# Attention scores of a head pair in one burst over four quadrants of TensorE, and a step later for the transposes

## The chip, the cores and the metric

The kernel runs on one core of one Trainium2 chip. The metric is the device time of one execution in microseconds (us), as the median of the runs; the profile shows one further execution. Engines: TensorE (PE; PEld is its weight load), VectorE (DVE), ScalarE (ACT), GpSimd (POOL) and SyncE (SP, which issues the DMAs).

## What is computed

Attention with two kinds of heads, then a feed-forward block with a gate, then a soft mixture of experts. Cut to what matters here:

```python
scores = scale * np.matmul(q, k.transpose(0, 1, 3, 2))      # 4 batches, 8 heads, 576 positions, 64 columns
mask_local   = (rel >= 0) & (rel < 32)                       # heads 0 to 3
mask_strided = (rel >= 0) & (pos[None, :] % 32 == pos[:, None] % 32)   # heads 4 to 7
attn = softmax(where(mask, scores, -1e9))
x = attn @ v                                                 # 2304 tokens, 512 columns
h = x @ w_in;  g = h * sigmoid(1.702 * h);  x = g @ w_out
...                                                          # slots: logits = x @ phi, experts, combination
```

## The kernel before

Everything is written out in Python loops, and the Tile framework gives each engine its fixed order, which follows the order of the calls except where it expects an operand too late.

**Chunks and steps.** The 2304 tokens are worked on in five chunks (four of 512, one of 256). A chunk has 16 steps, one for each 128 columns of the hidden layer. `moe_step` does a step: it advances the generators in `side` by one yield, lets `g_transpose` do 32 x 32 transposes on VectorE, and then `gemm1` (L321) fills the tile h_f with 12 products; ScalarE's tanh (L324) and a multiply on VectorE (L325) make g_f of it. Two h tiles are in PSUM at a time. After step f = 4, 8 and 12 (and step 0 of the next chunk) `logits` (L340) multiplies the last four g tiles. The tail of a chunk (`post`: the products lr, lp and u) runs in the first steps of the next.

**Attention beside it.** Batch b + 1 runs beside chunk b as a generator in `side` (`attention_steps`). A batch has four head pairs: pairs 0 and 1 are local, 2 and 3 strided. The two heads of a pair lie on partitions 0 to 63 and 64 to 127. The allowed positions are cut in units: 9 of 64 queries and 96 keys for a local pair, 11 of 64 x 64 for a strided one. The units are divided in two parts (5 + 4, 6 + 5). For each part `att_scores` computes the products (L163, two for a unit, one a head: row half h of TensorE into column half h), and then the softmax: mask and scale on VectorE (L166, from PSUM), maximum (L176), exponentials one unit at a time on ScalarE (L181), sum and reciprocal (L182, L183), and the normalisation on GpSimd (L184). `att_transpose` (L199) turns the probabilities of a pair on TensorE, and ScalarE copies them out (L203). `att_values` (L218) multiplies with V; ScalarE casts the result into the high part of x (L243), VectorE subtracts to get the low part (L244). For a strided pair the values of part 0 lie in row half 0 and those of part 1 in row half 1.

**The order around the change.** For batches 1 to 3 the sequence of steps is: scores 0.0, 0.1 (pair.part), then alternately the transposes or values of one pair and a score part of the next. Scores 0.0 and 0.1 both come in step 0 of the chunk; after that, a part, a transpose or values come in a step each. K and Q of a pair are loaded before its first part (two buffers), V before its transposes (one buffer). All small PSUM tiles (scores, transposes, values, lr, lp, u) come from the five buffers of `mtile`.

Of the kernel before, what the change touches and what calls it, by code (L numbers as in the profile page):

```python
# [18 lines left out]
B, H, S, D = 4, 8, 576, 64  # L19
# [5 lines left out]
QT, KL, NTL = 64, 96, 9  # L25
QS, KS, NTS = 3 * RA, 64, 11
SW = QS * (NTS - 1) + KS
HS = (NTS + 1) // 2
# [13 lines left out]
def tile_kernel(ctx: ExitStack, tc: tile.TileContext, lqk, lv, sqk, sv, wraw, phi, wexp, cst, out):  # L42
    nc = tc.nc
    P = 128
# [20 lines left out]
    def mtile(name):  # L65
        return ps_m.tile([P, 512], F32, tag="m", name=name)
# [22 lines left out]
    identb = att.tile([P, P], BF16, name="identb", bufs=1)  # L89
    maskb = att.tile([P, C_END - C_ML], BF16, name="maskb", bufs=1)  # L90
    maskL, maskL0, maskS = maskb[:, :KL], maskb[:, KL:2 * KL], maskb[:, 2 * KL:]
# [35 lines left out]

    probs, ptiles = {}, {}

    def att_scores(b, hp, part):  # L130
        t = qkv[b, hp]
        local = hp < 2
        nk, step = (KL, QT) if local else (KS, QS)
        ko = S if local else SW
        total, half = (NTL, 5) if local else (NTS, HS)
        u0, u1 = (0, half) if part == 0 else (half, total)
        nt = u1 - u0
        early = b == 0
        nm = f"{b}_{hp}_{part}"
        if part == 0:  # L140
            shape = [P, NTL if local else 2 * HS, nk]
            if b == 0 and hp >= 2:
                ts = ep.tile(shape, F32, name=f"ts_{b}_{hp}")
            else:
                ts = att.tile(shape, F32, tag="ts", name=f"ts_{b}_{hp}")
            probs[b, hp] = ts
            if not local:
                nc.gpsimd.memset(ts[:, NTS], 0.0)
        if local:
            ts = probs[b, hp][:, u0:u1]  # L150
        else:
            ts = probs[b, hp].rearrange("p (j e) k -> p e j k", e=2)[:, part, :nt]
        sp = mtile(f"s_{nm}")[:, :nt * nk].rearrange("p (u k) -> p u k", k=nk)
        mask = maskL if local else maskS
        if early:
            nc.tensor.matmul(sp, identb, mask.unsqueeze(1).to_broadcast([P, nt, nk]), start=True, stop=False)
            if local and part == 0:
                nc.tensor.matmul(sp[:, 0], identb, maskL0, start=False, stop=False)
        for u in range(nt):
            qo = step * (u0 + u)  # L160
            for h in range(2):
                hs = slice(64 * h, 64 * h + 64)
                nc.tensor.matmul(sp[hs, u], t[hs, qo:qo + 64], t[hs, ko + qo:ko + qo + nk], start=not early, stop=not early or u == nt - 1)  # L163

        def add_mask(a, z, m):
            nc.vector.scalar_tensor_tensor(ts[:, a:z], sp[:, a:z], SCALE, m.unsqueeze(1).to_broadcast([P, z - a, nk]), op0=ALU.mult, op1=ALU.add)  # L166

        if not early:
            if local and part == 0:
                add_mask(0, 1, maskL0)  # L170
                add_mask(1, nt, mask)
            else:
                add_mask(0, nt, mask)
        nmx = att.tile([P, 6], F32, tag="nmx", name=f"nmx_{nm}", bufs=4)
        src, sc = (sp, SCALE) if early else (ts, 1.0)
        nc.vector.tensor_reduce(nmx[:, :nt], src, axis=AX.X, op=ALU.max, negate=True)  # L176
        if early:
            nc.vector.tensor_scalar_mul(nmx[:, :nt], nmx[:, :nt], SCALE)
        sm = att.tile([P, 6], F32, tag="sm", name=f"sm_{nm}", bufs=4)
        for u in range(nt):  # L180
            nc.scalar.activation(ts[:, u], src[:, u], AF.Exp, scale=sc, bias=nmx[:, u:u + 1], accum_out=sm[:, u:u + 1])  # L181
        nc.vector.tensor_scalar_add(sm[:, :nt], sm[:, :nt], 1e-9)  # L182
        nc.vector.reciprocal(sm[:, :nt], sm[:, :nt])  # L183
        nc.gpsimd.tensor_tensor(ts, ts, sm[:, :nt].unsqueeze(2).to_broadcast([P, nt, nk]), op=ALU.mult)  # L184
# [20 lines left out]
    def att_values(b, hp):  # L205
        pt, v = ptiles.pop((b, hp)), vals[b, hp]
        local = hp < 2
        cut = 5 if local else HS
        av = [mtile(f"av_{b}_{hp}_{e}") for e in range(2)]

        def product(u, h):
            e, u0 = (0, u) if u < cut else (1, u - cut)
            if local:
                k0, nk, nq, o, w, p = 0, KL, QT, QT * u0, u, u
            else:
                k0, nk, nq, o, w, p = 64 * e, QS, min(QS, S - QS * u), QS * u0, u0, u0
                nk = nq
            nc.tensor.matmul(av[e][64 * h:64 * h + 64, o:o + nq], v[k0:k0 + nk, P * w + 64 * h:P * w + 64 * h + 64],  # L218
                             pt[k0:k0 + nk, p, 64 * h:64 * h + nq], start=True, stop=True)

        order = range(NTL) if local else [u for j in range(HS) for u in (j, j + HS) if u < NTS]
        for u in order:
            for h in range(2):
                product(u, h)
        for e in range(2):
            for c, (c0, cn) in enumerate(CHUNKS):
                if local:
                    s0 = S * b + QT * cut * e
                    n = QT * (cut, NTL - cut)[e]
                    lo, hi = max(s0, c0), min(s0 + n, c0 + cn)  # L230
                    if lo >= hi:
                        continue
                    src = av[e][:, lo - s0:hi - s0]
                    dsts = [x_tile(c)[k][:, hp, lo - c0:hi - c0] for k in range(2)]
                else:
                    a0, a1 = max(0, (c0 - S * b) // STR), min(RA, (c0 + cn - S * b) // STR)
                    if a0 >= a1:
                        continue
                    r0, nr = (0, 3 * HS) if e == 0 else (3 * HS, STR - 3 * HS)
                    lo = S * b + STR * a0 - c0  # L240
                    src = av[e][:, :RA * nr].rearrange("p (r a) -> p r a", a=RA)[:, :, a0:a1]
                    dsts = [x_tile(c)[k][:, hp, lo:lo + STR * (a1 - a0)].rearrange("p (a r) -> p r a", r=STR)[:, r0:r0 + nr, :] for k in range(2)]
                nc.scalar.copy(dsts[0], src)  # L243
                nc.vector.tensor_tensor(dsts[1], src, dsts[0].bitcast(F32), op=ALU.subtract)  # L244
# [261 lines left out]
    nc.vector.tensor_copy(identb, ident)  # L506
    nc.vector.tensor_scalar_mul(maskb, masks, 1.0 / SCALE)

    def attention_steps(b):
        la = 2 if b else 4  # L510
        order = list(range(la)) + [x for u in range(la, 8) for x in (la - 1 - u, u)] + list(range(la - 9, -9, -1))
        for x in order:
            if x >= 0:
                if b and x % 2 == 0:
                    load_qk(b, x // 2)
                att_scores(b, x // 2, x % 2)
                if b == 0:
                    keep_busy(1)
            else:
                x = -x - 1  # L520
                if x % 2:
                    att_values(b, x // 2)
                else:
                    if b:
                        load_v(b, x // 2)
                    att_transpose(b, x // 2)
                if b == 0:
                    keep_busy(4)
            yield

    for n, _ in enumerate(attention_steps(0)):
        if n in (8, 12):
            load_w(n // 4 - 2)
        if n == 10:
            split(0)
# [9 lines left out]

    for i, (c, f) in enumerate(steps):
        if f == 0 and c < 3:
            side.append(attention_steps(c + 1))
            next(side[-1])
        if (c, f) == (1, 0):  # L550
            raw_es.close()
            accp = acc_es.enter_context(tc.tile_pool(name="accp", bufs=1))
            sp_["p"] = accp
            acc = accp.tile([P, 4, 512], F32, name="acc")
            more = accp.tile([P, 3, 512], F32, name="more")
            slots.update({NF + 3 + k: more[:, k] for k in range(3)})
        if (c, f) == (3, 2):
            att_es.close()
            e1p = ctx.enter_context(tc.tile_pool(name="e1p", bufs=6, side="right"))
            for _ in range(6):  # L560
                load_ex(e1p, "e")
            for e in (1, 0, 1):
                load_ex(xp, f"x{e}")
        if (c, f) == (4, 1):
            for e in range(2):
                load_ex(xp, f"x{e}")
        moe_step(i)
        if (c, f) == (4, 4):
            for k in range(2):
                load_ex(None, gx_tile())  # L570
        if c == 4 and f % 2:
            load_ex(wip, "wi")
# [235 lines left out]
```

## Time and profile before

| | us |
|---|---|
| median of 3 runs | 438.43 (436.42 to 438.57) |
| profiled execution, its time | 439.01 |
| profiled execution, its span | 437.1 |
| PE busy | 411.6 |
| DVE busy | 263.6 |
| ACT busy | 194.1 |
| POOL busy | 77.5 |

The span goes from the first to the last instruction; the execution's own time also holds what lies around it. Busy time of PE counts pipelined products, so its share says that TensorE has work, not that it works at its peak. The mean granted clock is 0.985.

### The profile page before, as it was taken

How to read it: one execution, taken by the hardware profiler on the slowest of the kernel's cores; microseconds unless marked ns; L12 is line 12 of the kernel's file. 1: busy time of each engine (PE TensorE's matmuls, PEld its weight loads, DVE VectorE, ACT ScalarE, POOL GpSimd, SP SyncE). 2: the span in 40 equal slices, each digit the busy share in tenths (PEclk: the TensorE clock that was granted, in tenths of full speed). 3: DMA queues.
4: the chain of work that ended last, by engine and by line, in shares of the span. 5: the costliest groups of instructions: out<-in, count | busy, mean ns of one | idle time of the engine just before them, and what ended most of it. 6: DMA issues, size and time to landing. Idle time of an engine off the chain costs nothing.

```text
span 437.1 us, 10068 instructions
## 1 busy us (share of the span) xinstructions
PE 411.6 (94%) x4085; PEld 280.5 (64%) x4085; DVE 263.6 (60%) x564; ACT 194.1 (44%) x640; POOL 77.5 (18%) x96
## 2 busy tenths in 40 slices
PE   8978998998899999999999999999999999799992
PEld 4646575655467767777676776775777797243681
DVE  2789989998996555555557456546545465422141
ACT  3874867766664653555553436331221222220131
POOL 0454545454531110100110001000000000010000
PEclk9999999999989999999999999999999999899997
DMA  8957677676752130213411101693001899859998
GB/s 253 357 170 243 223 208 251 228 242 218 233 183 76 47 101 1 92 37 97 154 40 60 38 1 37 214 410 147 1 0 39 343 349 329 307 212 427 421 358 255
DMA packets 25614, 80.90 MB, mean 185 GB/s; under 512 B 2144, under 2 KB 9440, under 8 KB 21472
## 3 DMA queue, kind: packets, MB, share of 16 engines
q1 hardware_dynamic: 25568, 80.26, 52.5%
q8 instruction: 32, 0.52, 0.5%
q14 instruction: 14, 0.11, 0.1%
HBM read 71.34 MB, written 8.91 MB: 184 GB/s over the span
## 4 chain that ended last, share of the span: by engine, by line
PE 73%; DVE 8%; ACT 7%; POOL 4%; issue 3%; DMA 2%; SPq 0%; ACTq 0%; POOLq 0%; DVEq 0%
PE h L321 39%; PE u L435 5%; PE s L163 4%; PE lg L340 4%; PE op L671 4%; ACT ts L181 3%; PE hp L641 3%; PE ptp L199 3%; PE av L218 3%; DVE wc L264 2%; POOL ts L184 2%; PE fp L688 2%; POOL wc L262 2%; DVE wc L265 1%; DMA raw<-wraw 1%
## 5 line engine op out<-in xcount | busy, mean ns | idle before, releaser
L321 PE MATMUL h<-x,wi 128*128 128x512 f32 (+1 forms) x960 | 225.2, 381 | 4.3 <-POOL wi L273 1.7
L321 PEld LDWEIGHTS h<-x,wi 128*128 128x128 f32 x960 | 162.2, 189 | 53.8 <-issue 13.8
L325 DVE SCALAR_TENSOR_TENSOR gT<-gT,h 128x512 f32<-128x512 f32 (+1 forms) x64 | 40.6, 634 | 62.1 <-ACT gT L324 61.5
L324 ACT ACTIVATE gT<-h 128x512 f32<-128x512 f32 (+1 forms) x64 | 35.5, 555 | 68.2 <-PE h L321 66.6
L181 ACT ACTIVATE ts<-ts,nmx 128x64 f32<-128x64 f32 (+1 forms) x120 | 41.6, 349 | 28.6 <-DVE nmx L176 28.2
L184 POOL TENSOR_TENSOR ts<-ts,sm 128x384 f32<-128x384 f32 (+2 forms) x32 | 27.9, 872 | 139.2 <-DVE sm L183 65.5
L348 DVE STREAM_TRANSPOSE gT<-gT 128x512 f32<-128x512 f32 (+1 forms) x64 | 41.0, 649 | 0.9
L262 POOL TENSOR_SCALAR wc<-wc 128x512 f32<-128x512 f32 x32 | 25.0, 781 | 29.7 <-ACT wc L261 27.2
L340 PE MATMUL lg<-gT,wp 128*32 128x512 f32 (+1 forms) x128 | 27.2, 564 | 0.3 <-ACT wp L297 0.3
L264 DVE SCALAR_TENSOR_TENSOR wc<-raw,wc 128x512 uint32<-128x512 uint32 x32 | 26.0, 816 | 0.4
L263 DVE TENSOR_SCALAR wc<-wc 128x512 uint32<-128x512 uint32 x32 | 20.3, 635 | 7.9 <-POOL wc L262 7.9
L163 PE MATMUL s<-qk 64*64 64x96 f32 (+1 forms) x552 | 25.0, 235 | 0.0
L163 PEld LDWEIGHTS s<-qk 64*64 64x64 f32 x552 | 20.9, 133 | 6.3 <-issue 5.3
L243 ACT CAST x<-av 128x320 fp32r<-128x320 f32 (+20 forms) x54 | 19.1, 394 | 12.7 <-DVE x L244 9.1
L273 POOL TENSOR_TENSOR wi<-wc,wi 128x512 fp32r<-128x512 f32 x16 | 22.0, 1376 | 14.9 <-ACT wi L272 14.7
L265 DVE SCALAR_TENSOR_TENSOR wc<-raw,wc 128x512 uint32<-128x512 uint32 x32 | 24.4, 763 | 0.3
L261 ACT ACTIVATE wc<-raw 128x512 f32<-128x512 f32 x32 | 21.7, 678 | 4.3 <-DMA raw<-wraw 3.8
L182 DVE TENSOR_SCALAR sm<-sm 128x5 f32<-128x5 f32 (+2 forms) x32 | 6.8, 213 | 27.5 <-ACT ts L181 27.5
L435 PE MATMUL u<-gT,dT 32*32 32x512 f32 x576 | 21.0, 618 | 2.1 <-DVE z L410 2.1
L199 PE MATMUL ptp<-cs,ts 128*96 128x128 f32 (+1 forms) x120 | 18.2, 286 | 4.9 <-POOL ts L184 4.5
L181 ACT ACTIVATION_READ_ACCUMULATOR ts<-ts,nmx 128x1 f32 x120 | 22.6, 188 | 0.0
L699 POOL MEMSET hz<- 128x512 f32 x4 | 2.1, 560 | 112.1 <-PE spp L594 112.1
(124 smaller groups left out, 467.7 us busy)
## 6 DMA issues: line engine op xcount, KB each, us to landing
ex<-wexp SPq DMA_DIRECT2D x28, 1024.0 KB, 8.4
raw<-wraw SPq DMA_DIRECT2D x32, 512.0 KB, 4.2
qk<-lqk SPq DMA_DIRECT2D x8, 592.0 KB, 5.1
wo_scr<-wc SPq DMA_DIRECT2D x16, 256.0 KB, 2.8
ex<-wo_scr SPq DMA_DIRECT2D x4, 1024.0 KB, 9.2
gT<-wexp SPq DMA_DIRECT2D x4, 1024.0 KB, 7.0
qk<-sqk SPq DMA_DIRECT2D x6, 604.0 KB, 4.2
v<-lv SPq DMA_DIRECT2D x8, 432.0 KB, 4.8
```

The source lines that it names most:

```text
L163: nc.tensor.matmul(sp[hs, u], t[hs, qo:qo + 64], t[hs, ko + qo:ko + qo + nk], start=not early, stop=not early or u == nt - 1)
L181: nc.scalar.activation(ts[:, u], src[:, u], AF.Exp, scale=sc, bias=nmx[:, u:u + 1], accum_out=sm[:, u:u + 1])
L184: nc.gpsimd.tensor_tensor(ts, ts, sm[:, :nt].unsqueeze(2).to_broadcast([P, nt, nk]), op=ALU.mult)
L199: nc.tensor.transpose(ptp[:nk, u - a], src, ident)
L262: nc.gpsimd.tensor_scalar(t, t, F64_LARGE, F64_SMALL, op0=ALU.min, op1=ALU.max)
L264: nc.vector.scalar_tensor_tensor(u, raw[:, :, 1], 0xC0000000, u, op0=ALU.bitwise_and, op1=ALU.bitwise_or)
L321: nc.tensor.matmul(h[:, :N], w[:, we, 128 * kt:128 * kt + 128], x[xe][:, kt, :N], start=n == 0, stop=n == 11)
L324: nc.scalar.activation(g[:, :N], h[:, :N], AF.Tanh, scale=0.851)
L325: nc.vector.scalar_tensor_tensor(g[:, :N], g[:, :N], 1.0, h[:, :N], op0=ALU.add, op1=ALU.mult)
L340: nc.tensor.matmul(lgs[c][32 * j:32 * j + 32, :N], wp[:, f0 + j, :], gs[c, f0 + j][:, :N], start=f0 == 0, stop=f0 == NF - 4)
L348: nc.vector.transpose(t_slots(c)[:, f, :N], gs[c, f][:, :N])
L435: nc.tensor.matmul(us[a][32 * j:32 * j + 32, :].rearrange("p (t f) -> p t f", f=32), dT[q, 32 * b:32 * b + 32], gT[q, :, 32 * b:32 * b + 3 ...
```

## The change

- For batches 2 and 3 a new generator `attention_pairs` takes the place of `attention_steps` (now `attention_units`, which still serves batches 0 and 1). Steps of a pair: values of the pair before, scores of both parts, softmax of part 0; softmax of part 1, loads of V and of the next K and Q; a free step (not for pair 3); transposes.
- `att_scores` can issue both parts at once, unit by unit: part 0 and part 1 alternate. Part 1 writes head h into column half 1 - h, so that the four products of a turn use four different quadrants.
- The softmax is a function of its own, `att_softmax`, with the same operations. In part 1 of every batch the heads now stand exchanged in the rows of the probabilities, and so in the columns after the transposes; `att_values` reads them accordingly (`h ^ e`, where e is 1 for the second part of a strided pair).
- K and Q of the first pair of batch 2 are loaded in batch 1's step of the last transposes.

```diff
-    def att_scores(b, hp, part):
+    def att_scores(b, hp, parts=(0, 1)):
...
+        for u in range(half):
+            for part in parts:
+                if part * half + u >= total:
+                    continue
+                qo = step * (part * half + u)
+                for h in range(2):
+                    hs, o = slice(64 * h, 64 * h + 64), 64 * (h ^ part)
+                    nc.tensor.matmul(sp[part][o:o + 64, u], t[hs, qo:qo + 64], t[hs, ko + qo:ko + qo + nk], start=not early, stop=not early or part * half + u in (half - 1, total - 1))
...
-        for u in range(nt):
-            qo = step * (u0 + u)
-            for h in range(2):
-                hs = slice(64 * h, 64 * h + 64)
-                nc.tensor.matmul(sp[hs, u], t[hs, qo:qo + 64], t[hs, ko + qo:ko + qo + nk], start=not early, stop=not early or u == nt - 1)
...
-                             pt[k0:k0 + nk, p, 64 * h:64 * h + nq], start=True, stop=True)
+                             pt[k0:k0 + nk, p, 64 * (h ^ e):64 * (h ^ e) + nq], start=True, stop=True)
...
+                    if (b, x) == (1, 6):
+                        load_qk(2, 0)
...
+    def attention_pairs(b):
+        for hp in range(4):
+            if hp:
+                att_values(b, hp - 1)
+            att_scores(b, hp)
+            att_softmax(b, hp, 0)
+            yield
+            att_softmax(b, hp, 1)
+            load_v(b, hp)
+            if hp < 3:
+                load_qk(b, hp + 1)
+            yield
+            if hp < 3:
+                yield
+            att_transpose(b, hp)
+            yield
+        att_values(b, 3)
+        if b < 3:
+            load_qk(b + 1, 0)
+        yield
...
-            side.append(attention_steps(c + 1))
+            side.append((attention_pairs if c else attention_units)(c + 1))
```

Below is the order of the instructions at three places of batch 2, beside chunk 1. Names: s_pair_part are scores, av values, ptp transposes, pt their copy, ts probabilities, h_f and gT or more the tiles of the gemm, lg the logits, x_2 and x_3 the gemm's operands. In the first two blocks TensorE at step 3. Before, the end of h_3 and what followed it:

```order
L321 MATMUL h_3_1983<-x_1_308,wi_740 128x512
L321 MATMUL h_3_1983<-x_1_307,wi_740 128x512
L163 MATMUL s_1_1_1998<-qk_1_1898 64x96 x8
L435 MATMUL u_0_2018<-gT,dT_1936 32x512 x4
L435 MATMUL u_1_2019<-gT,dT_1936 32x512 x4
```

Now, from the values ahead of h_3 on (the turns go on to the fifth of part 0, and then h_3 comes):

```order
L233 MATMUL av_0_0_1930<-pt_0_1884,v_0_1843 64x64 x10
L233 MATMUL av_0_1_1931<-pt_0_1884,v_0_1843 64x64 x8
L165 MATMUL s_1_0_1959<-qk_1_1845 64x96 x2
L165 MATMUL s_1_1_1960<-qk_1_1845 64x96 x2
L165 MATMUL s_1_0_1959<-qk_1_1845 64x96 x2
L165 MATMUL s_1_1_1960<-qk_1_1845 64x96 x2
```

Part 1 came behind h_3, and part 0 ahead of h_2, a step before the values; now the two parts stand together, in turns, between the values and h_3.

ScalarE in steps 9 to 12, before and now:

```order
L324 ACTIVATE gT<-h_9_2302 128x512
L181 ACTIVATE ts_3_2319,sm_3_0_2337<-ts_3_2319,nmx_3_0_2335 128x64 x6
L324 ACTIVATE gT<-h_10_2348 128x512
L243 CAST x_2_896<-av_2_0_2363 128x18x12
L243 CAST x_2_896<-av_2_1_2364 128x14x12
L243 CAST x_3_1979<-av_2_0_2363 128x18x6
L243 CAST x_3_1979<-av_2_1_2364 128x14x6
L324 ACTIVATE gT<-h_11_2396 128x512
L181 ACTIVATE ts_3_2319,sm_3_1_2425<-ts_3_2319,nmx_3_1_2423 128x64 x5
L324 ACTIVATE more<-h_12_2435 128x512
```

Now:

```order
L339 ACTIVATE gT<-h_10_2320 128x512
L258 CAST x_2_896<-av_2_1_2336 128x14x12
L258 CAST x_2_896<-av_2_0_2335 128x18x12
L258 CAST x_3_1954<-av_2_0_2335 128x18x6
L258 CAST x_3_1954<-av_2_1_2336 128x14x6
L196 ACTIVATE ts_3_2367,sm_3_0_2396<-ts_3_2367,nmx_3_0_2394 128x64 x6
L339 ACTIVATE gT<-h_11_2407 128x512
L196 ACTIVATE ts_3_2367,sm_3_1_2425<-ts_3_2367,nmx_3_1_2423 128x64 x5
L339 ACTIVATE more<-h_12_2437 128x512
```

The six exponentials of part 0 stood ahead of tanh of h_10, a step before the casts; now they stand behind the casts and ahead of tanh of h_11.

TensorE at step 13, before and now:

```order
L340 MATMUL lg_2105<-gT,wp 32x512 x3
L321 MATMUL h_13_2468<-x_1_307,wi_1521 128x512
L321 MATMUL h_13_2468<-x_1_308,wi_1521 128x512
L321 MATMUL h_13_2468<-x_1_307,wi_1521 128x512 x2
L321 MATMUL h_13_2468<-x_1_308,wi_1521 128x512
L199 MATMUL ptp_3_0_2457<-cs,ts_3_2319 128x128 x3
L199 MATMUL ptp_3_1_2462<-cs,ts_3_2319 128x128 x3
```

Now:

```order
L355 MATMUL lg_2109<-gT,wp 32x512 x3
L336 MATMUL h_13_2468<-x_1_307,wi_1521 128x512
L214 MATMUL ptp_3_0_2457<-cs,ts_3_2367 128x128 x3
L214 MATMUL ptp_3_1_2462<-cs,ts_3_2367 128x128 x3
L336 MATMUL h_13_2468<-x_1_308,wi_1521 128x512
```

The transposes of pair 3 stood behind five products of h_13, now behind one (in batch 3 behind three).

## Rows read from the trace of the kernel before

**Rows 1.** The page, part 1: busy time, share of the span, instructions.
```profile
PE 411.6 (94%) x4085; PEld 280.5 (64%) x4085; DVE 263.6 (60%) x564; ACT 194.1 (44%) x640; POOL 77.5 (18%) x96
```

**Rows 2.** Stretches of chunks 1 and 2: busy us of engines, granted clock, DMA share.
```profile
138.20:209.90 71.70, 71.70 (x713) 51.93 (x712) 40.20 (x90) 35.20 (x128) 7.04 (x10) 1.00 0.19 59
209.90:283.00 73.10, 72.93 (x720) 52.89 (x720) 42.13 (x93) 34.08 (x125) 7.04 (x10) 1.00 0.23 75
```

**Rows 3.** Chain of waits in order of time: start, us until the next, what.
```profile
148.30 0.97 PE s L163 x20
...
158.12 0.81 PE s L163 x16
...
171.18 0.84 PE s L163 x24
...
174.97 1.20 PE av L218 x36
176.17 2.95 PE h L321 x12
179.12 0.73 PE s L163 x20
...
182.79 0.99 PE lg L340 x8
```

**Rows 4.** Timeline of PE: start, us, engine, line, operation, count.
```profile
187.44 0.91 PE L163 MATMUL s<-qk 64*64 64x64 f32 x24
...
191.25 0.91 PE L218 MATMUL av<-pt,v 54*64 54x54 f32 x44
192.09 3.01 PE L321 MATMUL h<-x,wi 128*128 128x512 f32 x12
...
201.00 0.87 PE L199 MATMUL ptp<-cs,ts 128*128 128x128 f32 x6
...
209.91 1.70 PE L163 MATMUL s<-qk 64*64 64x96 f32 x36
211.55 3.03 PE L321 MATMUL h<-x,wi 128*128 128x512 f32 x12
```

**Rows 5.** Timeline of ACT, steps 10 to 12 of chunk 1.
```profile
190.48 0.35 ACT L181 ACTIVATE ts<-ts,nmx 128x64 f32<-128x64 f32 x1 [2.34 <-DVE nmx L176]
...
192.49 0.58 ACT L324 ACTIVATE gT<-h 128x512 f32<-128x512 f32 x1
192.97 0.87 ACT L243 CAST x<-av 128x216 fp32r<-128x216 f32 x2
...
197.88 0.35 ACT L181 ACTIVATE ts<-ts,nmx 128x64 f32<-128x64 f32 x1 [2.14 <-DVE nmx L176]
...
199.55 0.58 ACT L324 ACTIVATE more<-h 128x512 f32<-128x512 f32 x1
```

**Rows 6.** Timeline of DVE, steps 10 and 11 of chunk 1.
```profile
188.18 0.69 DVE L325 SCALAR_TENSOR_TENSOR gT<-gT,h 128x512 f32<-128x512 f32 x1 [2.57 <-ACT gT L324]
188.78 0.55 DVE L166 SCALAR_TENSOR_TENSOR ts<-s,maskb 128x384 f32<-128x384 f32 x1
189.25 0.70 DVE L348 STREAM_TRANSPOSE gT<-gT 128x512 f32<-128x512 f32 x1
189.88 0.51 DVE L176 TENSOR_REDUCE nmx<-ts 128x6 f32<-128x384 f32 x1
...
193.10 0.69 DVE L325 SCALAR_TENSOR_TENSOR gT<-gT,h 128x512 f32<-128x512 f32 x1
193.70 0.93 DVE L244 TENSOR_TENSOR x<-av,x 128x216 fp32r<-128x216 f32 x2
...
195.77 0.69 DVE L325 SCALAR_TENSOR_TENSOR gT<-gT,h 128x512 f32<-128x512 f32 x1
```

**Rows 7.** Timeline of POOL, the normalisation of pair 3's part 1 in batch 2.
```profile
200.22 0.72 POOL L184 TENSOR_TENSOR ts<-ts,sm 128x320 f32<-128x320 f32 x1 [6.23 <-ACT more L324]
```

More of the change, by code (lines that the diff above doesn't have):

```diff
@@ L128, in tile_kernel, with att_units @@
     probs, ptiles = {}, {}
-    def att_scores(b, hp, part):
+    sps = {}
+    def att_units(hp):
+        local = hp < 2
+        return (KL, QT, S, NTL, 5, maskL) if local else (KS, QS, SW, NTS, HS, maskS)
+    def att_scores(b, hp, parts=(0, 1)):
         t = qkv[b, hp]
         local = hp < 2
[L133 to L137, printed above, removed]
+        nk, step, ko, total, half, mask = att_units(hp)
         early = b == 0
-        nm = f"{b}_{hp}_{part}"
-        if part == 0:
-            shape = [P, NTL if local else 2 * HS, nk]
+        shape = [P, NTL if local else 2 * HS, nk]
+        if (b, hp) not in probs:
             if b == 0 and hp >= 2:
@@ L148, in att_scores, with att_softmax @@
                 nc.gpsimd.memset(ts[:, NTS], 0.0)
+        sp = sps.setdefault((b, hp), {})
+        for part in parts:
+            nt = (half, total - half)[part]
+            sp[part] = (mtile(f"s_{b}_{hp}_{part}")[:, :nt * nk].rearrange("p (u k) -> p u k", k=nk))
+            if early:
+                nc.tensor.matmul(sp[part], identb, mask.unsqueeze(1).to_broadcast([P, nt, nk]), start=True, stop=False)
+                if local and part == 0:
+                    nc.tensor.matmul(sp[0][:, 0], identb, maskL0, start=False, stop=False)
+        for u in range(half):
+            for part in parts:
+                if part * half + u >= total:
[4 more added lines that the diff above has]
+                    nc.tensor.matmul(sp[part][o:o + 64, u], t[hs, qo:qo + 64], t[hs, ko + qo:ko + qo + nk], start=not early, stop=not early or part * half + u in (half - 1, total - 1))
+    def att_softmax(b, hp, part):
+        local = hp < 2
+        nk, step, ko, total, half, mask = att_units(hp)
+        u0, u1 = (0, half) if part == 0 else (half, total)
+        nt = u1 - u0
+        early = b == 0
+        nm = f"{b}_{hp}_{part}"
+        sp = sps[b, hp][part]
         if local:
@@ L152, in att_scores @@
             ts = probs[b, hp].rearrange("p (j e) k -> p e j k", e=2)[:, part, :nt]
[L153 to L158, printed above, removed]
-        for u in range(nt):
-            qo = step * (u0 + u)
-            for h in range(2):
-                hs = slice(64 * h, 64 * h + 64)
-                nc.tensor.matmul(sp[hs, u], t[hs, qo:qo + 64], t[hs, ko + qo:ko + qo + nk], start=not early, stop=not early or u == nt - 1)
         def add_mask(a, z, m):
@@ L507, in tile_kernel, with attention_units @@
     nc.vector.tensor_scalar_mul(maskb, masks, 1.0 / SCALE)
-    def attention_steps(b):
+    def attention_units(b):
         la = 2 if b else 4
@@ L515, in attention_steps @@
                     load_qk(b, x // 2)
-                att_scores(b, x // 2, x % 2)
+                att_scores(b, x // 2, (x % 2,))
+                att_softmax(b, x // 2, x % 2)
                 if b == 0:
@@ L529, in attention_steps @@
             yield
-    for n, _ in enumerate(attention_steps(0)):
+    def attention_pairs(b):
[18 more added lines that the diff above has]
+        yield
+    for n, _ in enumerate(attention_units(0)):
         if n in (8, 12):
```

## The prediction

> **What bounds the kernel now.** I start with the page: TensorE is busy for 411.6 of 437.1 us [rows 1], so it is the first suspect. An average over the span says nothing of the stage that is changed, so the second view is the table of stretches. Batches 2 and 3 are computed in the stretches from 138.20 and from 209.90 us, beside the gemms of chunks 1 and 2. In the first TensorE is busy for all of its 71.70 us, in the second for 72.93 of 73.10 [rows 2]; VectorE and ScalarE are busy for about half. The granted clock is 1.00 in both, the upper level (2.4 GHz), and as TensorE stays busy I see no reason for it to move. So here a microsecond less of TensorE is one off the end, as long as nothing else becomes late. Later loads of expert weights are released by buffers that TensorE frees, so they move with it.
>
> The third view, the chain of waits in order of time, gives the price of each burst from its start to the next one: 0.84 and 0.73 us for the two score bursts of a strided pair, 0.97 and 0.81 for a local one, 2.95 for the 12 products of an h tile, 0.99 for four logit products, 1.20 for the values of a local pair [rows 3]. The records count double: 22 products of a strided pair show as 24 + 20 records.
>
> The fourth view is TensorE's timeline. The values of a strided pair already go to four quadrants: two row halves (parts 0 and 1) by two column halves (the heads). These 44 records of 54 columns take 0.84 us, from 191.25 to 192.09 [rows 4]. The scores of the same pair use two quadrants, the diagonal, and take 1.57 for 44 records. That contrast is the whole case for the change.
>
> **Part one: the bursts.** Removed: the four strided pairs (two in each of two batches) cost 4 x (0.84 + 0.73) = 6.28 us. Three local pairs cost 0.97 + 0.81 = 1.78 each, and the local pair 0 of batch 3, whose 36 records stand together, takes 1.64 (209.91 to 211.55) [rows 4]; together 6.98. Sum 13.26 us.
>
> Added: the same products in eight bursts over four quadrants. No row has such scores, so I bound them by the values row, 19 ns a record (0.84 / 44).
> - Strided, 64 columns: from 0.84 (if a record costs the same whatever its columns) to 0.84 x 64/54 = 1.00.
> - Local, 96 columns, 36 records: from 36 x 19 ns = 0.69 to 0.69 x 96/54 = 1.22.
>
> Inside these: with two quadrants a record costs 35 ns at 64 columns (0.84 / 24) and 45.6 at 96 (1.64 / 36), so 10.6 more for 32 columns. Four quadrants should show half of that, 5.3 ns. From 54 to 64 columns that adds 1.7 ns (20.8 x 44 = 0.91 us), from 54 to 96 it adds 7 (26 x 36 = 0.94). Sum 4 x 0.91 + 4 x 0.94 = 7.4. **Gain 13.26 - 7.4 = 5.9 us**, by the bounds 13.26 - 8.9 = 4.4 up to 13.26 - 6.1 = 7.1.
>
> Both heads of one part still write into one bank from different row halves, as they do now. Now a record costs 35 ns at 64 columns, and the values of a local pair, which have no row halves and two column halves, cost 33 (1.20 / 36) [rows 3]. So two row halves on one bank show no price. The Trainium skill, "TensorEngine Tiling (Array Packing)", section "Gotcha 1: PSUM Pressure", says that different row tiles cannot access the same bank simultaneously; if they took turns, each of the two banks would serve one row half at a time and the gain would be 0 instead of 5.9. The bursts of now should suffer from that already and do not; its case is rival A.
>
> **Part two: what becomes late.** The softmax of part 0 used to stand a step earlier than that of part 1. Now both follow one burst, ahead of tanh of the h tile of that step on ScalarE, and of the multiply that makes g on VectorE. In step 11 the casts of the values of pair 2 come before both. I walk through step 11 of batch 2, with 0 at the end of h_10.
>
> VectorE: the multiply behind tanh starts 0.74 after TensorE has left the h tile (187.44 to 188.18), the next operation 0.60 later, a transpose takes 0.63 (189.25 to 189.88) [rows 4, 6]; so the subtractions start at 1.97. Four subtractions and a transpose take 2.07 (193.70 to 195.77), so the four take 1.44. The mask of part 0 stands among them, 0.47 (188.78 to 189.25). The maximum starts at 1.97 + 1.44 + 0.47 = 3.88. ScalarE: its exponentials start 0.60 after that (189.88 to 190.48), six take 2.01 (190.48 to 192.49) [rows 5, 6]: 6.49. Then tanh, the multiply 0.61 later (192.49 to 193.10), 0.69 long: g_11 is there at 7.79. TensorE: values 0.84, scores 0.91, two h tiles 5.90: the logits, which need g_11, come at 7.65. **Wait 0.15.** Then the five exponentials of part 1: start 0.48 after tanh did (192.49 to 192.97) at 6.97, 1.67 long (197.88 to 199.55), and 0.67 later GpSimd's normalisation (200.22), 0.72 long [rows 5, 7]: 10.03. TensorE has done the logits at 8.8, and by the new order it comes to the transposes after a single product of h_13, at 9.05. **Wait 1.0.** Before, they stood after five products, and came (201.00) when GpSimd had just finished (200.94).
>
> Batch 3 has all four subtractions and both masks first, so g_11 comes 0.4 later: wait 0.55 at the logits, and at the transposes, after three products of h_13, another 0.55. Sum of these waits 0.15 + 1.0 + 0.55 + 0.55 = 2.25, **taken as 2.3 us**. Bounds: 0, if VectorE or ScalarE overlap the pieces better, and 4.5, if each piece is late by half a microsecond more.
>
> In step 7 there are three subtractions or two of a local pair, not four, and the values take 1.20: by the same steps g_7 comes at about 7.7 and TensorE at 8.0. No wait, with 0.3 to spare. Step 3 has the u products of the chunk before behind h_3, which need nothing of this softmax and cover it; the logits come after them and h_4.
>
> **The rest costs nothing that shows.** The free step lets the transposes of pairs 0 to 2 start a step later, with the softmax long done; it takes away at most the 0.17 us that TensorE shows idle in the second stretch [rows 2]. Splitting the score function changes no instruction. The earlier calls of the loads (in batch 1 too) change no row on SP's queue, and none on GpSimd's; V of a pair still waits for the values of the pair before, three steps ahead of its use. The score tiles take two of five PSUM buffers at once; what held them was read a step earlier, so nobody queues.
>
> **Sum.** The profiled execution took 439.01 us, 437.1 of it span: 439.0 - 5.9 + 2.3 = 435.4. It stands 0.6 above the median of the runs, 438.43; against that the result is **434.9 us**, 0.8% faster.
>
> **Rivals.**
> A. The four quadrants give nothing: the two row halves share each bank and take turns. For it: the values rows have one bank per row half, the scores will not. Against it: the diagonal bursts share a bank at full pace. TensorE then comes to the logits and transposes later by the 0.7 us that the burst did not save (5.9 / 8): the waits at the logits go, and about 0.5 is left at the transposes of each batch, where the order now has them one or three products into h_13 and not five: 438.4 + 1.0 = **439.4 us, slower**. It decides from the point where the eight bursts together save less than 1 us.
> B. The gain is there and the waits are not: the four subtractions are done sooner than I have them, or the bursts end near their upper bound so that TensorE comes later anyway. 438.4 - 5.9 = **432.5 us**.
> C. The gain is there and step 7 stalls like step 11 (spare only 0.3): two waits at the logits of 0.5 and later exponentials, waits 4.5: 438.4 - 5.9 + 4.5 = **437.0 us**, no difference that can be told.
> That the change does not do what it says can be left aside: the order shows the two parts alternating.
>
> **How the numbers follow.** The case of the sum 0.60, B 0.22, C 0.11, A 0.07. A run of this kernel can tell about 0.5% from no change, 2.2 us: the line is 436.2. The sum's own range, with the bounds of the bursts, is 433.4 to 436.4 (the low gain of 4.4 with 2.3 of waits is 436.3), a little of it beyond the line; B lies before it, C beyond, A on the other side but within 0.5% mostly. Faster 0.78, same 0.18, slower 0.04. The range reaches from B with the high gain cut by half a microsecond of waits, 438.4 - 7.1 + 0.5 = 431.8, to C, 437.0.
>
> **What would show it.** Right: the eight bursts show 36 or 44 records in 0.85 to 1.0 us; TensorE waits for the logits after h_12 and for the transposes of pair 3 on GpSimd, some 2 us in all; the stretches of chunks 1 and 2 shrink by 3 to 4 us and later ones keep their length. Wrong: bursts of 1.5 us (A), no idle TensorE in the two stretches (B), a wait for g_7 at the logits after h_8 (C). A stretch of another chunk that changes by more than half a microsecond would be none of my cases.

## The result and the profile after

The changed kernel takes **431.79 us** (median of 4 runs, 430.23 to 433.18), the kernel before 438.28 beside it (4 runs, 436.42 to 438.57). The ratio is 0.9853, with a 95% interval of 0.9828 to 0.9879: 6.5 us faster, where the forecast was 3.5. The forecast range (from 431.8) ends at this time. The profiled execution took 433.18 us, 431.4 of it span, against 439.01 and 437.1.

The page, part 1, answers to [rows 1]:

```profile
PE 403.6 (94%) x4080; PEld 275.2 (64%) x4085; DVE 266.3 (62%) x564; ACT 193.6 (45%) x640; POOL 77.9 (18%) x96
```

TensorE is busy for 8.0 us less, and the span is 5.7 shorter: some of the gain became idle time. To see where, I take one stretch in both traces, from the first score burst of batch 2 to the logits in step 0 of chunk 3. In the kernel before it goes from 138.19 to 284.27, **146.08 us**. Here it is cut in two where batch 3 begins (us, then busy time with the count for TensorE, weight load, VectorE, ScalarE, GpSimd; granted clock; share and rate of the DMAs), and answers to [rows 2]:

```profile
138.00:207.00 69.00, 68.25 (x716) 49.71 (x715) 41.09 (x90) 34.86 (x128) 7.04 (x10) 1.00 0.21 61
207.00:278.74 71.74, 71.04 (x726) 51.55 (x725) 43.82 (x94) 33.84 (x125) 7.04 (x10) 1.00 0.25 83
```

Together **140.74 us**, 5.34 less than before, at the granted clock 1.00 (the upper level) in both. TensorE is idle for 1.45 of it, before for 0.17. So 5.3 of the profiled 5.8 us come from where the change was made.

The new bursts in the chain of waits (start, us until the next, what), which answer to [rows 3]:

```profile
153.07 0.97 PE s L165 x36
...
171.98 1.20 PE av L233 x36
173.18 0.84 PE s L165 x44
174.03 5.66 PE h L336 x24
179.68 1.00 PE lg L355 x8
...
191.59 2.10 ACT ts L196 x12
193.69 0.48 ACT gT L339
194.18 1.67 ACT ts L196 x10
...
196.41 0.72 POOL ts L199
197.18 0.87 PE ptp L214 x6
```

A local pair's 36 records take 0.97 us, a strided pair's 44 take 0.84. The chain leaves TensorE in the lower rows: twelve records of exponentials (six of them), tanh, five more exponentials, the normalisation, and only then the transposes. That is the wait which the prediction walked through, and its two places stand in TensorE's timeline (start, us, engine, line, operation, count, idle time before it and its releaser), as in [rows 4]:

```profile
186.97 0.84 PE L233 MATMUL av<-pt,v 54*64 54x54 f32 x41
...
188.51 5.74 PE L336 MATMUL h<-x,wi 128*128 128x512 f32 x24
194.18 0.62 PE L355 MATMUL lg<-more,wp 128*32 128x512 f32 x1
...
194.64 1.36 PE L355 MATMUL lg<-gT,wp 128*32 128x512 f32 x4
195.92 0.51 PE L336 MATMUL h<-x,wi 128*128 128x512 f32 x1
197.18 0.87 PE L214 MATMUL ptp<-cs,ts 128*128 128x128 f32 x6 [0.75 <-POOL ts L199]
197.81 2.75 PE L336 MATMUL h<-x,wi 128*128 128x512 f32 x11
200.49 0.91 PE L233 MATMUL av<-pt,v 54*64 54x54 f32 x44
...
264.42 1.05 PE L355 MATMUL lg<-gT,wp 128*32 128x512 f32 x2 [0.23 <-DVE gT L340]
265.39 0.96 PE L336 MATMUL h<-x,wi 128*128 128x512 f32 x3
266.65 0.87 PE L214 MATMUL ptp<-cs,ts 128*128 128x128 f32 x6 [0.29 <-POOL ts L199]
```

Idle time alone understates these waits. The logits of step 12 of chunk 1 last from 194.18 to 195.92, 1.74 us, where eight such records take 1.00 elsewhere. Nothing is shown as idle there: records that wait for g_11 are drawn as long ones (1.36). I therefore count a wait as the time from the start of one group to the next, less what the same group takes undisturbed.

### The profile page after: what moved, and what is told of

Read it like the earlier page. It is cut to its first block, busy times and chain, and to the rows that moved or that the text cites. A ratio compares the mean times of both kernels' runs of the same rounds, so it can differ in the third digit from the quotient of the medians.

```text
span 431.4 us, 10062 instructions
## 1 busy us (share of the span) xinstructions
PE 403.6 (94%) x4080; PEld 275.2 (64%) x4085; DVE 266.3 (62%) x564; ACT 193.6 (45%) x640; POOL 77.9 (18%) x96
## 4 chain that ended last, share of the span: by engine, by line
PE 70%; ACT 10%; DVE 9%; POOL 5%; issue 3%; DMA 1%; SPq 0%; ACTq 0%; POOLq 0%; DVEq 0%
PE h L336 37%; ACT ts L196 5%; PE u L450 5%; PE lg L355 4%; PE op L710 4%; PE hp L680 3%; PE s L165 3%; PE ptp L214 2%; POOL ts L199 2%; PE av L233 2%; DVE wc L279 2%; PE fp L727 2%; POOL wc L277 2%; ACT wc L276 1%; DVE x L259 1%
## 5 line engine op out<-in xcount | busy, mean ns | idle before, releaser
L336 PE MATMUL h<-x,wi 128*128 128x512 f32 (+1 forms) x960 | 222.1, 379 | 4.1 <-POOL wi L288 1.7
L355 PE MATMUL lg<-gT,wp 128*32 128x512 f32 (+1 forms) x128 | 28.6, 564 | 0.5 <-ACT wp L312 0.3
L279 DVE SCALAR_TENSOR_TENSOR wc<-raw,wc 128x512 uint32<-128x512 uint32 x32 | 27.0, 845 | 0.4
L280 DVE SCALAR_TENSOR_TENSOR wc<-raw,wc 128x512 uint32<-128x512 uint32 x32 | 24.4, 762 | 0.3
L339 ACT ACTIVATE more<-h 128x512 f32<-128x512 f32 (+1 forms) x16 | 8.6, 536 | 28.2 <-PE h L336 28.2
L259 DVE TENSOR_TENSOR x<-av,x 128x320 fp32r<-128x320 f32 (+20 forms) x54 | 19.9, 392 | 1.8 <-ACT x L258 1.5
L214 PEld LDWEIGHTS ptp<-cs,ts 128*96 128x96 f32 (+1 forms) x120 | 12.8, 132 | 12.8 <-POOL ts L199 11.5
```

The source lines that it names most:

```text
L214: nc.tensor.transpose(ptp[:nk, u - a], src, ident)
L279: nc.vector.scalar_tensor_tensor(u, raw[:, :, 1], 0xC0000000, u, op0=ALU.bitwise_and, op1=ALU.bitwise_or)
L336: nc.tensor.matmul(h[:, :N], w[:, we, 128 * kt:128 * kt + 128], x[xe][:, kt, :N], start=n == 0, stop=n == 11)
L339: nc.scalar.activation(g[:, :N], h[:, :N], AF.Tanh, scale=0.851)
L355: nc.tensor.matmul(lgs[c][32 * j:32 * j + 32, :N], wp[:, f0 + j, :], gs[c, f0 + j][:, :N], start=f0 == 0, stop=f0 == NF - 4)
```

## The experiments

For each, the stretch named above is given beside the time, because it repeats better. In a second profile of the unedited changed kernel it took 140.73 us, against 140.74 in the first, while the two executions took 430.54 and 433.18. Whole runs scatter by 1.5 us and more.

**1. Two quadrants instead of four.**

```diff
-                    hs, o = slice(64 * h, 64 * h + 64), 64 * (h ^ part)
+                    hs, o = slice(64 * h, 64 * h + 64), 64 * h
...
-                             pt[k0:k0 + nk, p, 64 * (h ^ e):64 * (h ^ e) + nq], start=True, stop=True)
+                             pt[k0:k0 + nk, p, 64 * h:64 * h + nq], start=True, stop=True)
```

> The changed kernel with both heads of part 1 in the same column halves as in part 0, so that a burst uses two quadrants and not four; order, merging and free step stay. Theory Q (four quadrants make the burst short): strided bursts of 44 records take about 1.45 us and local ones of 36 about 1.6, as the two-quadrant pitch of before gives, against 0.7 to 0.85 and 0.97 in the changed kernel; some 5.3 us more of TensorE, of which about 2 come back because TensorE then comes later to g_11 and to the transposes of pair 3: 435 us. Theory M (the merging of the two bursts alone does it): as the changed kernel, 431.8 us.

Measured: 436.67 us (10 runs; before 438.23, 13 runs), ratio 0.9954 (0.9937 to 0.9971). The stretch takes 143.95 us, 3.2 more than with four quadrants. The bursts of pairs 1 and 2 in TensorE's timeline:

```profile
153.82 1.70 PE L165 MATMUL s<-qk 64*64 64x96 f32 x36
174.60 1.50 PE L165 MATMUL s<-qk 64*64 64x64 f32 x44
```

From start to next they take 1.64 and 1.43 us, against 0.97 and 0.85. Over the eight bursts the quadrants are worth 4 x 0.67 + 4 x 0.58 = 5.0 us. Of these 1.7 are given back in waits, which are shorter here since TensorE comes later: 1.15 at the logits of step 12 (1.16 and 1.69 us instead of 1.74 and 2.26) and the rest at the transposes of local pairs. Rival A has fallen. And a kernel with two quadrants is still 2.1 us shorter in the stretch than the one before, though its bursts (4 x 1.64 + 4 x 1.43 = 12.3) are only 1.0 cheaper and it waits: something else gains.

**2. Four quadrants, the parts one after the other.** Part 0's products first, then part 1's.

```diff
-        for u in range(half):
-            for part in parts:
+        for part in parts:
+            for u in range(half):
```

> The changed kernel with all products of part 0 and then all of part 1: the four quadrants are used in a burst, but only two of them in turn at a time. If the turns of four are what counts: bursts as with two quadrants, 1.45 and 1.6 us, time about 435 us. If it is enough that a burst touches four quadrants: 431.8 us.

Measured: 435.0 us (4 runs), 0.9925 (0.9903 to 0.9947); stretch 142.31. The bursts:

```profile
154.06 1.44 PE L165 MATMUL s<-qk 64*64 64x96 f32 x36
174.61 1.33 PE L165 MATMUL s<-qk 64*64 64x64 f32 x44
```

From start to next they take 1.37 and 1.26 us, between the two cases of the expectation. How many records of the burst from 153.00 (changed kernel), 153.82 (two quadrants) and 154.06 (in sequence) touch a fifth of a microsecond shows why. A record is drawn 0.24 us long in all three runs, so the count (in brackets) goes with the pace at which records start:

```profile
153.20:153.40 0.20, 0.20 (x20) 1.00 0.00 0
```

```profile
154.02:154.22 0.20, 0.20 (x10) 1.00 0.00 0
```

```profile
154.26:154.46 0.20, 0.20 (x10) 1.00 0.00 0
154.66:154.86 0.20, 0.20 (x17) 1.00 0.38 82
```

Alternating, 20 records; on the diagonal, 10; in sequence 10 at first and up to 17 in the middle of the burst. I read the 17 as part 0's last products beside part 1's first; the trace does not tell the two parts apart. So it is the turn of four different quadrants that doubles the pace within the burst; the same quadrants used one diagonal after the other bring about a third of the saving (1.70 to 1.44, against 1.04).

**3. Without the free step.**

```diff
-            if hp < 3:
-                yield
```

> The changed kernel without the free step: the transposes of a pair are called in the step after its second softmax, and all later pairs come a step or more earlier. If the free step is needed: TensorE waits for GpSimd's normalisation at most of the eight sets of transposes, 1 us or more each, and the time is 436 us or more. If it only shifts the waits: the logits after h_8 and h_12 come with their g tiles long done (1.9 us less of waits), the transposes split h tiles or wait half a microsecond each, 430 to 432 us.

Measured: 435.37 us (4 runs), 0.993 (0.9913 to 0.9947); stretch 144.20, 3.5 more. Waits of TensorE from 136 to 283 us (what waited for what: us in total, times, longest):

```profile
PE ptp L214 <- POOL ts L199: 3.9, 4, 1.5
PE h L336 <- DVE gT L340: 0.9, 1, 0.9
PE ptp L214 <- DVE sm L197: 0.6, 1, 0.6
```

Five times in eight TensorE comes to the transposes before the probabilities are ready; the expectation had most of the eight, with 1 us or more each, and a time of 436. The free step is needed: it keeps pairs 0 and 2 from such waits (0.6 us each here), while pair 3, which has no free step in either kernel, waits 1.5 and 1.3. The prediction credited it with the 0.17 us that were idle before, and did not ask what the joined softmax would cost without it.

**4. The free step moved from pair 1 to pair 3.**

```diff
-            if hp < 3:
+            if hp != 1:
```

> The changed kernel with the free step taken from pair 1 and given to pair 3: the scores of pairs 2 and 3 come at steps 6 and 10, two steps ahead of the logits, and the transposes of pair 3 have a step more. If the lost time in steps 12 and 13 of both chunks is a wait for the softmax that stands ahead of tanh (some 3.5 us in the changed kernel by its chain): it goes, 428 to 429 us, and logits take 1.0 us everywhere. If that time is lost for another reason: 431.8 us.

Measured: 432.74 us (429.88 to 433.38, 4 runs), 0.9863 (0.9828 to 0.9898); stretch 139.95, only 0.8 less than the changed kernel. The waits at the logits of step 12 and at pair 3's transposes are gone, and another has come, here in the list of waits and in the timeline of batch 2:

```profile
PE h L336 <- DVE gT L340: 2.0, 2, 1.3
```

```profile
191.20 3.06 PE L336 MATMUL h<-x,wi 128*128 128x512 f32 x12 [0.70 <-DVE gT L340]
```

An h tile now waits until the multiply behind tanh has freed the buffer that it writes to; tanh of that earlier tile stands behind the six exponentials of part 0 on ScalarE. The step between logits and transposes did not cure the cause, it moved the wait: the exponentials ahead of tanh. The expectation of 428 to 429 us was wrong in that.

**5. The kernel before, with part 1's scores joined to the values.** No quadrants and no free step: in batches 2 and 3 of the old kernel, part 1 of pairs 1 to 3 is issued right behind the values of the pair before, and its own step is left empty.

```diff
+            if b > 1 and x in (3, 5, 7):
+                yield
+                continue
...
+                    if b > 1 and x // 2 < 3:
+                        att_scores(b, x // 2 + 1, 1)
```

> The kernel before, in which only the place of six bursts changes: in batches 2 and 3 the scores of part 1 of pairs 1 to 3 stand right behind the values of the pair before and no longer alone between two h tiles. Same products, two quadrants, same softmax. If each place where TensorE goes from an h tile to products on quadrants and back costs some 0.2 us beside the burst (in the trace 24 products of h in a row take 5.67 us, and 12 beside such a place 2.95 each): six places fewer, 1.2 to 1.8 us, 436.7 us. If a burst costs its own time alone: no change, 438.2 us.

Measured: 437.76 us (12 runs; before 438.83, 17 runs), 0.9974 (0.9953 to 0.9995); stretch 145.45, 0.63 less than before, where 1.2 to 1.8 was expected. The logits of step 12 now wait in both batches (197.37 to 198.97, 1.60 us instead of 1.0), which hides 1.2; without it the stretch would be 1.8 shorter, though not one product has changed. Pairs 2 and 3 of batch 2 in TensorE's timeline:

```profile
176.23 5.76 PE L321 MATMUL h<-x,wi 128*128 128x512 f32 x24
181.92 0.62 PE L340 MATMUL lg<-more,wp 128*32 128x512 f32 x1
...
182.91 0.87 PE L199 MATMUL ptp<-cs,ts 128*128 128x128 f32 x6
183.54 3.02 PE L321 MATMUL h<-x,wi 128*128 128x512 f32 x12
...
191.71 5.74 PE L321 MATMUL h<-x,wi 128*128 128x512 f32 x24
197.37 0.62 PE L340 MATMUL lg<-more,wp 128*32 128x512 f32 x1
...
198.97 0.87 PE L199 MATMUL ptp<-cs,ts 128*128 128x128 f32 x6
```

Two h tiles with no burst between them take 5.69 and 5.66 us until the logits; with one between they were 2.95 + 2.94. A place where TensorE leaves the h tiles for products on quadrants costs 0.2 us besides the burst itself.

The edit moves more than the six bursts, however: the softmax of part 1 comes a step earlier with them, and the transposes of pairs 2 and 3 now stand ahead of an h tile and no longer inside it. In the kernel before, those of pair 2 split the tile:

```profile
183.72 1.42 PE L321 MATMUL h<-x,wi 128*128 128x512 f32 x5
185.01 0.87 PE L199 MATMUL ptp<-cs,ts 128*128 128x128 f32 x6
185.64 1.87 PE L321 MATMUL h<-x,wi 128*128 128x512 f32 x7
```

The two pieces took 1.29 + 1.80 us (the next group came at 187.44), the whole tile takes 2.95 (183.54 to 186.49). Of the 1.8 us, 0.8 lie in the four places where two h tiles now stand together (pair 1's bursts have the u products behind them in both kernels), 0.6 in the four sets of transposes, and 0.3 in pair 3's bursts, which are joined to the values of pair 2.

**6. The exponentials called behind the gemm.** As in experiment 4, and the exponentials, sums and normalisation of pairs 2 and 3 in batches 2 and 3 are put in a list that is run behind the first gemm of the step, so that its tanh is called ahead of them.

```diff
+        def exps():
...
+        if b > 1 and hp > 1:
+            late.append(exps)
+        else:
+            exps()
...
         gemm1(c, f)
+        while late:
+            late.pop(0)()
...
-            if hp < 3:
+            if hp != 1:
                 yield
```

> The kernel of the moved free step, in which the exponentials of pairs 2 and 3 of batches 2 and 3 are issued behind the gemm of their step, so that ScalarE's order has tanh of the h tile ahead of most of them. If what was left in that kernel (2.0 us of TensorE waiting for an h buffer at h_12) is the softmax in front of tanh: the waits go, the stretch from the first score burst of batch 2 to the logits in step 0 of chunk 3 falls from 139.95 to about 138.0 us, and the time to 427 to 430. If another chain holds the h buffer: 139.95 and no gain.

Measured: **429.84 us** (428.8 to 432.25, 6 runs; before 438.83), 0.9782 (0.9747 to 0.9818); stretch 138.71, 2.0 less than the changed kernel and 1.2 less than experiment 4 (138.0 was expected). What is left of the waits:

```profile
PE h L345 <- DVE gT L349: 0.7, 2, 0.4
PE ptp L223 <- POOL ts L203: 0.6, 2, 0.5
```

Not all six exponentials went behind tanh: five still stand ahead of it in batch 2 and three in batch 3. The chain of waits through the place shows it, with two records for an exponential, first in experiment 4 (batch 2), then here (both batches):

```profile
187.84 2.10 ACT ts L196 x12
189.94 0.49 ACT gT L339
```

```profile
190.85 1.77 ACT ts L200 x10
192.62 0.49 ACT gT L348
...
259.24 1.11 ACT ts L200 x6
260.35 0.48 ACT gT L348
```

One exponential fewer ahead of tanh shortens the wait for the buffer in batch 2 from 0.70 to 0.37 us, three fewer shorten it in batch 3 from 1.31 to 0.32: 0.33 for each, which is what one takes. So the exponentials ahead of tanh were its cause. The sums on VectorE moved as well, but the multiply starts 0.6 us behind the start of tanh in both runs. This version beats both kernels.

**7. The changed kernel again**, beside experiments 5 and 6.

> The changed kernel itself, unedited, on the same chip as the two others: 431.8 us, stretch from the first score burst of batch 2 to the logits in step 0 of chunk 3 140.74 us.

Measured: 432.35 us (430.54 to 434.17, 6 runs), 0.9842 (0.9806 to 0.9877), the first result again; stretch 140.73. Experiment 6 is 2.5 us faster on the same chip; the stretch shows 2.0 of it.

## Why the prediction was half right

**The bursts: right.** The local ones cost 0.97 each (forecast 0.94), pair 2's 0.84 and 0.85. Pair 3's stand joined to the values, 1.54 together (186.97 to 188.51), less 0.84 for the values alone: 0.70 (forecast 0.91). Sum 4 x 0.97 + 0.84 + 0.85 + 2 x 0.70 = 7.0, a gain of 13.26 - 7.0 = **6.3 us** (forecast 5.9).

**Rival A: refuted**, and with it what the Trainium skill says in "TensorEngine Tiling (Array Packing)", "Gotcha 1: PSUM Pressure", that different row tiles cannot access the same bank at once, as far as it would have them take turns here. Both heads of a part write into one bank from two row halves, and 44 records take the same 0.84 us as the values do with a bank for each row half [rows 4]. That alone could be a floor, since 54 and 64 columns cost the same. Experiment 1 closes it: there the two parts also alternate between two banks, so if row halves took turns on a bank, the second product of part 0 could run beside the first of part 1, and two quadrants would be as fast as four. They take 1.43 us, not 0.85.

**The chain behind the softmax: right.** Counted from the end of h_10, as in the prediction, g_11 was there at 7.93 in batch 2 (194.21 + 0.69 - 186.97; forecast 7.79), and the transposes could start at 10.21 (197.18 - 186.97; the normalisation was forecast to end at 10.03). These are the rows of ScalarE, VectorE and GpSimd for it, as in [rows 5 to 7]:

```profile
193.60 0.57 ACT L339 ACTIVATE gT<-h 128x512 f32<-128x512 f32 x1
```

```profile
194.21 0.69 DVE L340 SCALAR_TENSOR_TENSOR gT<-gT,h 128x512 f32<-128x512 f32 x1
```

```profile
196.41 0.72 POOL L199 TENSOR_TENSOR ts<-ts,sm 128x320 f32<-128x320 f32 x1 [1.31 <-ACT more L339]
```

In batch 3 the logits could go on at 8.50 (264.42 - 255.92; forecast 7.79 + 0.4 = 8.19), the transposes at 10.73.

**The step that failed: "The rest costs nothing that shows", and with it the price of a burst "from its start to the next one".** That price leaves out what a burst costs the h tiles beside it. I charged each h tile 2.95 us wherever it stood; but the trace of before had a row that says otherwise, in which TensorE goes through two tiles without a break:

```profile
204.25 5.73 PE L321 MATMUL h<-x,wi 128*128 128x512 f32 x24
```

The next burst starts at 209.91 [rows 4]. That is 5.66 for two, not 5.90. The change makes fewer such places: both parts go in one burst, from pair 1 on behind the values of the pair before, and the transposes of pairs 0 to 2 stand between whole h tiles instead of inside one. Summed from start to next over all h rows of the stretch, and less idle time and waits, the h tiles took 97.8 us before and 95.0 after; the transposes took 0.5 more, and small groups 0.3 less. So some **2.6 us** came from a term that I had at nothing. Experiment 5 shows 1.5 us of it in the h tiles, with the old bursts, and experiment 1 has it as the gain that two quadrants could not explain. The Trainium skill has a rule that fits, in "TensorEngine Tiling (Array Packing)", "Key Properties": a change of tiling mode drains TensorE. The rows show a price for such an excursion, 0.2 us; that it is the drain, and not something else at the seam, no run here separates. Against the drain as the whole cause stands that the transposes of pairs 2 and 3, which are 128*128 in their rows like the h tiles, also cost an h tile 0.15 us where they split it (experiment 5).

**The waits: right place, wrong size.** From the start of h_11 to the values of pair 3 it takes 11.98 us in batch 2 (188.51 to 200.49) and 12.07 in batch 3. Undisturbed it would be 5.67 + 1.00 + 0.63 + 2.93 = 10.23: two h tiles, logits, transposes, one h tile. Waits of 1.75 + 1.84 = **3.6 us**, forecast 2.3. The waits at the transposes are as forecast: 1.0 and 0.6 us. Those at the logits are 0.74 and 1.26 instead of 0.15 and 0.55. TensorE came to them at 7.21 (194.18 - 186.97) where I had 7.65, since the joined burst and the two h tiles took 1.54 + 5.67 and not 0.84 + 0.91 + 5.90: 0.44 earlier in each batch, half of it by the cheaper burst, half by the same missing term. The rest, 0.15 and 0.3, is g_11 that came later than walked. One more wait was not forecast, since I took the softmax of pairs 0 to 2 to be "long done": the transposes of pair 0 take 1.16 and 1.35 us (146.00 to 147.16 and 214.78 to 216.13), against 0.98 in experiment 1, as they wait for the normalisation of part 1. This 0.55 us is the 0.5 that the transposes took more above, so the missing term is nearer 3 us, and the waits are nearer 4 than 3.6.

**The sum of the stretch:** -6.3 - 2.6 + 3.6 = -5.3, measured -5.34, forecast -5.9 + 2.3 = -3.6. So 1.7 of the miss is explained by this place. The profiled execution was 2.2 us below its forecast (433.18 against 435.4), and the median 3.1. The span ahead of the stretch and the one behind it are each 0.2 shorter (138.00 against 138.19, 152.66 against 152.83); that and the lower median lie within the scatter of whole runs. That the time falls on the lower end of the range is luck: this end stood for bursts that gain 7.1 and waits of 0.5, and the bursts gained 6.3 and the waits were 3.6, made up for by a term that was not in the sum.

**Rival B** gave nearly the time, 432.5, for another reason: it had no waits, and there are 3.6 us of them. **Rival C** did not come: the logits behind h_8 take their usual 1.0 us (179.68 in the chain, x8).

## What to carry to other kernels

Price small products on quadrants by the whole neighbourhood: look in the trace for the same big tiles with and without them between, and put such bursts side by side. When products get faster, recompute when their engine reaches the next thing it waits for; a part of the gain stays there, and more of it is got back in the order of the other engine (here exponentials behind tanh, 1.2 us) than by moving a free step (0.8). And issue products so that neighbours in the order fall on different quadrants, since using all four is not enough.

## What the runs showed of the hardware

- Four quadrants in turn: 44 records of 64 columns take 0.84 us, as long as 44 of 54 columns do, 19 ns each. I had expected 1.7 ns more a record. With 96 columns it is 27 ns (0.97 / 36; expected 26).
- Two diagonals one after the other: 1.33 to 1.44 us instead of 0.9 to 1.0 for the same products, alternating.
- Two h tiles in a row: 5.66 us, not 2 x 2.95. An h tile split by transposes: 3.09 us, whole 2.95.
- A product that waits in the middle of a group may be drawn as a long record and not as idle time: 1.45 us of idle time in the stretch stand for some 4.1 us of waits (3.6 in steps 12 and 13, 0.55 at the transposes of pair 0).
